# A fused attention and feed-forward kernel: one written-out order of operations for the whole first chunk

## The chip, the core and the metric

The kernel runs as one program on one core of a Trainium2 chip. The metric is the device time of one execution in microseconds. The engines named here are TensorE (PE, with its weight loads as PEld), VectorE (DVE), ScalarE (ACT), GpSimd (POOL) and SyncE (SP), which here issues nearly all DMA transfers. Each engine works through its own queue in the order in which the program hands instructions out; an instruction that waits for another engine holds up all that stand behind it on its own.

## The reference

Sparse attention over 4 batches of 8 heads, 576 positions and 64 columns a head, and then two feed-forward layers over the 2304 resulting rows of 512 columns:

```
def _attn_ref(q, k, v):
    scores = (1.0 / np.sqrt(D)) * np.matmul(q, k.transpose(0, 1, 3, 2))
    # heads 0-3 see the last 32 positions, heads 4-7 every 32nd position
    scores = np.where(masks[None], scores, -1000000000.0)
    attn = np.exp(scores - np.max(scores, axis=-1, keepdims=True))
    attn = attn / (np.sum(attn, axis=-1, keepdims=True) + 1e-09)
    return np.matmul(attn, v)

h = x @ w_in                      # 512 -> 2048
x = (h - np.tanh(h)) @ w_out      # 2048 -> 512
g = x @ w_gate                    # 512 -> 1536
x = (g / (1.0 + np.exp(-g)) * (x @ w_val)) @ w_out2
```

The inputs are float32; q and k are drawn eight times larger than in the base recipe.

## The kernel before

The 2304 rows are cut into five chunks, four of 512 and one of 256. The first feed-forward layer runs chunk by chunk, and while one chunk is multiplied, the attention of the next batch is computed beside it. The second layer follows and isn't touched by the change.

**Attention in groups.** A batch has 4 pairs of heads, and a pair 3 groups of 3 blocks of 64 queries: 12 groups a batch. Groups 0 to 11 are batch 0, groups 12 to 23 batch 1. A group goes through `scores` (PE: small matmuls), `top` (DVE: mask and row maximum, into SBUF), `exp` (ACT), `recip` (DVE), `mult` (POOL, or ACT in three instructions), `turn` (PE: three transposes into PSUM), `bring` (a copy of 384 columns from PSUM to SBUF, DVE or ACT), `value` (PE: small matmuls) and `keep` (ACT: a copy to SBUF). For groups 13 to 23 all `scores` write one part of a PSUM bank, all `turn` a second and all `value` a third, so each waits for the reader of the one before it.

**Weights in pieces.** The first layer's weights arrive as 32 pieces of 64-bit words and are turned into float32 by steps on three engines: `words` (SP: the load, into one of five buffers), `high` and `low` (ACT), `bound` (two DVE instructions, L177 and L181), `join` (POOL, L188), `sign` (DVE, L192), `head` (ACT, L198) and `rest` (POOL, L201). The last two split each weight into a high and a low part; a product takes three matmuls of 512 columns (high by high, low by high, high by low). Piece steps are the largest item on DVE and POOL in the first chunk.

**The first chunk.** Column block f of the hidden layer (f from 0 to 15) takes `first` (PE, 12 matmuls into a bank), `tanh` (ACT), `less` (DVE), `gh` (ACT) and `gl` (DVE), and then `second` (PE, 12 matmuls into four accumulators, the first eight of which read `gh` alone). This, the groups of batch 1 and the pieces are interleaved, which I call a round for each f.

**What sets the order.** Two things before the change. The text `BEGIN` is a list of such operations, written `verb.index.option`; `Opening.run` reads it word by word and hands the instructions out in that order (`warm.12` is twelve idle-time matmuls on PE; `ready` the same into a bank that a group will use; `part`, `half` and `first.i.f.n` are matmuls of the first layer; `.P`, `.V` and `.A` name POOL, DVE and ACT). It covers batch 0, and f up to 4. From f = 5 (`FROM`) the loop over `f` at the end of the kernel takes over with a fixed order: normalise the last group, `first`, `tanh`, `less`, a `value`, a `scores`, a tick of the piece feed, `second` of f-1, a `turn` and its `bring`, `gh`, `gl`, `exp`, and a second tick. A tick (`Feed.tick`) does `high` and `low` of one piece, `bound` and `join` of the one before and `sign`, `head`, `rest` of the one before that. In both, the sums of `second` for f = 15 are left to the end of the chunk, after the inputs of chunk 1 have been split.

The functions of `Opening` that read the list, and the loop:

Of the kernel before, what the change touches and what calls it, by code (L numbers as in the profile page):

```python
# [63 lines left out]
BEGIN = """
scores.0 top.0 exp.0.n warm.12 recip.0 mult.0.P keys.0.1 scores.1 scores.2 top.1 turn.0 top.2 exp.1.c queries.0.1
values.0.0 recip.1 warm.6 exp.2.n warm.6 words.0 keys.0.2 scores.3 scores.4 bring.0.V recip.2 mult.1.P turn.1 top.3
mult.2.P exp.3.c value.0 top.4 keep.0 queries.0.2 mask bring.1.V turn.2 scores.5 value.1 exp.4.n warm.12 bring.2.V
top.5 recip.3 mult.3.P recip.4 turn.3 keep.1 piece.0.high mult.4.P exp.5.c value.2 piece.0.low keep.2 piece.0.bound
bring.3.V turn.4 high.2 scores.6 bring.4.V recip.5 top.6 scores.7 values.0.1 words.1 top.7 scores.8 exp.6.n
piece.0.join piece.0.sign exp.7.c value.3 recip.6 piece.1.high mult.5.P low.2 turn.5 warm.12 keep.3 piece.1.low  # L70
bring.5.V words.2 ready.99.2 recip.7 top.8 exp.8.n mult.7.P warm.6 piece.1.bound value.4 keep.4 turn.7 keys.0.3
queries.0.3 mult.6.P bring.7.V turn.6 value.5 recip.8 piece.1.join piece.1.sign piece.0.head piece.2.high keep.5
scores.10 values.0.2 scores.9 scores.11 bring.6.V value.6 mult.8.P high.3 piece.0.rest ready.8.6 turn.8 low.3
piece.1.head words.3 xh.6 piece.1.rest top.9 top.10 exp.10.n values.0.3 xl.6 value.7 piece.2.bound words.4 words.5
keys.1.0 recip.10 top.11 ready.9.6 exp.9.c recip.9 mult.9.P xh.7 xl.7 piece.3.high mult.10.P ready.11.2 part.0.2
part.0.3 bring.8.V exp.11.c piece.3.low part.1.2 piece.3.bound recip.11 value.8 xh.8 left.8 xl.8 turn.9 turn.10
bring.9.V mult.11.A bring.10.V part.1.3 piece.3.join queries.1.0 value.9 values.1.0 keys.1.1 piece.2.low queries.1.1
piece.2.join xh.9 piece.4.high turn.11 piece.3.sign piece.3.head xl.9 part.0.0 bring.11.V value.10 value.11
piece.5.high xh.10 xh.11 piece.4.bound part.1.0 values.1.1 xl.11 left.11 first.3.2.1 xl.10 piece.4.low piece.5.low
words.6 scores.12 piece.2.sign piece.2.head piece.3.rest piece.5.bound half.0.0 half.0.1 words.7 piece.4.join tanh.0  # L80
top.12 piece.2.rest half.1.0 less.0 scores.13 half.1.1 first.3.2.11 piece.4.sign exp.12.c top.13 gh.0 gl.0
piece.5.join exp.13.c scores.14 second.2.0.8 tanh.1 piece.5.sign piece.5.head recip.12 recip.13 tanh.2 words.8 words.9
piece.4.head second.2.0.4 mult.12.P mult.13.P top.14 less.1 gh.1 second.4.1.1 less.2 piece.6.high gl.1 piece.5.rest
piece.6.rebase turn.12 piece.4.rest exp.14.c piece.6.low bring.12.V piece.7.high piece.7.low first.5.3.12 recip.14
piece.8.high piece.8.low piece.7.bound value.12 gh.2 scores.15 piece.6.join piece.6.sign piece.6.head top.15 exp.15.c
piece.9.high gl.2 tanh.3 mult.14.P turn.13 second.4.1.7 piece.7.join words.10 words.11 spill.5 piece.8.bound
piece.7.sign second.4.1.4 piece.6.rest recip.15 piece.8.join bring.13.V piece.9.bound second.6.2.8 piece.8.sign
keep.12 value.13 piece.7.head keys.1.2 queries.1.2 piece.7.rest piece.10.high mult.15.P piece.9.low scores.16
piece.9.join turn.14 less.3 second.6.2.4 bring.14.V top.16 words.12 gh.3 first.7.4.1 piece.10.bound keep.13
piece.9.sign gl.3 first.7.4.11 turn.15 bring.15.V piece.8.head piece.8.rest piece.10.low words.13 second.8.3.1  # L90
piece.11.low piece.11.high tanh.4 second.8.3.11 piece.10.join piece.11.bound words.14 piece.10.sign piece.9.head
piece.9.rest spill.8 exp.16.c less.4 piece.12.high piece.10.head words.15 gh.4 piece.11.join piece.13.high
# [1660 lines left out]
```

## Time and profile before

| | us |
|---|---|
| median of three runs | 866.4 (866.13 to 866.54) |
| the profiled execution | 866.65 |
| its span, first to last instruction | 864.8 |
| PE busy in the span | 858.8 |
| DVE busy | 639.5 |
| ACT busy | 463.5 |
| POOL busy | 334.9 |

Times in the rows below are counted from the start of the span. An engine's busy time is the union of its instructions as the profiler records them; ends of matmuls are modelled, and matmuls overlap, so a row of PE is read by the start of the next one. The opening lasts to about 28 us, where the first wide matmul starts; chunk 0 ends on PE at 138.43 us.

### The profile page before, as it was taken

The page shows a single profiled execution, that of the slowest core. Times are in us where ns is not written, and L with a number is a line of the kernel's source. Part 1 is how long each engine was busy: PE and PEld are TensorE (multiplying, and loading weights), DVE is VectorE, ACT ScalarE, POOL GpSimd, SP SyncE. Part 2 cuts the span into 40 slices and gives each one's busy share as a digit, 9 for nine tenths or more (in the row PEclk, how much of TensorE's full clock was granted, in tenths as well). Part 3 has the DMA queues.
Part 4 walks back from the last instruction along what each step waited for, and adds up shares of the span by engine and source line. Part 5 has one row for each costly group of instructions (what it writes and reads, how often), then busy time and mean ns, then how long its engine had stood idle before and what let it go on. Part 6 is the DMA issues. An engine that isn't in the chain of part 4 may idle for free.

```text
span 864.8 us, 13917 instructions
## 1 busy us (share of the span) xinstructions
PE 858.8 (99%) x4782; PEld 720.3 (83%) x4782; DVE 639.5 (74%) x1218; ACT 463.5 (54%) x1059; POOL 334.9 (39%) x284
## 2 busy tenths in 40 slices
PE   9999999999999999999999999999999999999998
PEld 7877778888888889998888888888888888888886
DVE  6999996688867785248887887888777867785451
ACT  6988874534343524237644655655454446854531
POOL 3889994754546550005125214463553310000000
PEclk9999999999999999999999999999999999999999
DMA  9967646530352213247356436453444458978651
GB/s 267 293 236 243 197 165 203 211 98 25 128 191 91 74 50 122 98 150 250 137 171 217 148 121 199 145 196 143 160 159 170 165 203 307 372 250 274 197 186 42
DMA packets 67253, 152.47 MB, mean 176 GB/s; under 512 B 7600, under 2 KB 14128, under 8 KB 67184
## 3 DMA queue, kind: packets, MB, share of 16 engines
q1 hardware_dynamic: 66752, 151.35, 52.1%
q8 instruction: 37, 0.61, 0.3%
q10 hardware_dynamic: 432, 0.25, 0.1%
q14 instruction: 32, 0.26, 0.1%
HBM read 108.06 MB, written 43.52 MB: 175 GB/s over the span
## 4 chain that ended last, share of the span: by engine, by line
PE 89%; ACT 5%; DVE 4%; issue 1%; DMA 0%; POOL 0%; SPq 0%; POOLq 0%
PE ps_acc L627 17%; PE ps_h L252 8%; PE ps_h L251 8%; PE ps_h L253 8%; PE ps_acc L253 8%; PE ps_acc L252 8%; PE ps_acc L251 8%; PE ps_a L252 5%; PE ps_a L251 5%; PE ps_a L253 5%; PE ps_acc L1626 2%; DVE m L192 2%; ACT s L368 1%; PE ps_a L414 1%; PE ps_a L343 1%
## 5 line engine op out<-in xcount | busy, mean ns | idle before, releaser
L627 PE MATMUL ps_acc<-gh,w 128*128 128x512 f32 (+1 forms) x546 | 124.8, 370 | 0.0
L188 POOL TENSOR_TENSOR sl<-sl,st 128x512 int32<-128x512 int32 x36 | 51.4, 1434 | 164.9 <-PE ps_acc L627 73.6
L251 PE MATMUL ps_acc<-sl 128*128 128x512 f32 x288 | 112.1, 389 | 0.0
L252 PE MATMUL ps_acc<-sl 128*128 128x512 f32 x288 | 112.1, 389 | 0.0
L253 PE MATMUL ps_acc<-sl 128*128 128x512 f32 x288 | 112.0, 389 | 0.0
L627 PEld LDWEIGHTS ps_acc<-gh,w 128*128 128x128 f32 x546 | 94.1, 189 | 16.0
L1213 DVE TENSOR_TENSOR sl<-sl 128x512 fp32r<-128x512 f32 (+1 forms) x120 | 71.7, 660 | 22.9 <-ACT sl L1209 22.9
L251 PE MATMUL ps_h<-xh,w 128*128 128x512 f32 (+1 forms) x226 | 85.1, 376 | 0.0
L252 PE MATMUL ps_h<-xh,w 128*128 128x512 f32 (+1 forms) x226 | 84.4, 374 | 0.1
L253 PE MATMUL ps_h<-xl,w 128*128 128x512 f32 (+1 forms) x226 | 84.2, 372 | 0.0
L1209 ACT CAST sl<-sl 128x512 fp32r<-128x512 f32 (+1 forms) x120 | 66.1, 599 | 23.9 <-DMA sl<-gd 18.2
L607 ACT ACTIVATE t<-ps_h 128x512 f32<-128x512 f32 (+1 forms) x54 | 30.4, 563 | 83.2 <-PE ps_h L253 83.2
L466 POOL TENSOR_TENSOR pr<-skv,sq 128x576 f32<-128x576 f32 (+8 forms) x40 | 57.4, 1461 | 44.5 <-DVE sc L473 31.5
L627 PE MATMUL ps_acc<-gl,w 128*128 128x512 f32 (+1 forms) x273 | 67.1, 366 | 0.0
L608 DVE TENSOR_TENSOR ps_h<-ps_h,t 128x512 f32<-128x512 f32 (+1 forms) x54 | 35.5, 657 | 40.3 <-ACT t L607 40.0
L253 PEld LDWEIGHTS ps_acc<-sl 128*128 128x128 f32 x288 | 54.1, 188 | 11.2
L252 PEld LDWEIGHTS ps_acc<-sl 128*128 128x128 f32 x288 | 54.1, 188 | 11.1
L251 PEld LDWEIGHTS ps_acc<-sl 128*128 128x128 f32 x288 | 54.1, 188 | 11.0
L466 POOL TENSOR_TENSOR pr<-skv,sc 128x576 f32<-128x576 f32 (+8 forms) x40 | 45.9, 1164 | 37.7 <-DVE xo L473 28.1
L251 PE MATMUL ps_a<-sl 128*128 128x512 f32 x144 | 56.1, 390 | 0.0
L252 PE MATMUL ps_a<-sl 128*128 128x512 f32 x144 | 56.1, 390 | 0.0
L253 PE MATMUL ps_a<-sl 128*128 128x512 f32 x144 | 56.0, 389 | 0.0
(207 smaller groups left out, 2096.3 us busy)
## 6 DMA issues: line engine op xcount, KB each, us to landing
st<-in_w SPq DMA_DIRECT2D x68, 512.0 KB, 4.5
gd<-t SPq DMA_DIRECT2D x84, 256.0 KB, 2.2
sl<-gd SPq DMA_DIRECT2D x84, 256.0 KB, 4.7
w<-w1s SPq DMA_DIRECT2D x32, 512.0 KB, 3.5
w3s<-sl SPq DMA_DIRECT2D x24, 256.0 KB, 3.2
sl<-w3s SPq DMA_DIRECT2D x24, 256.0 KB, 5.3
x2d<-o SPq DMA_DIRECT2D x17, 256.0 KB, 2.7
w1s<-w SPq DMA_DIRECT2D x8, 512.0 KB, 5.3
```

The lines of the kernel that those rows point to most:

```text
L188: nc.gpsimd.tensor_tensor(out=mi, in0=mi, in1=self.lo, op=ALU.add)
L192: nc.vector.scalar_tensor_tensor(out=mi, in0=self.hi, scalar=-2 ** 30, in1=mi, op0=ALU.bitwise_and, op1=ALU.bitwise_or,)
L251: nc.tensor.matmul(ps, lhsT=wh, rhs=xh, start=start, stop=False, skip_group_check=goes_on)
L252: nc.tensor.matmul(ps, lhsT=wl, rhs=xh, start=False, stop=False, skip_group_check=goes_on)
L253: nc.tensor.matmul(ps, lhsT=wh, rhs=xl, start=False, stop=stop, skip_group_check=goes_on)
L466: nc.gpsimd.tensor_tensor(out=t, in0=x, in1=y, op=ALU.mult)
L607: nc.scalar.activation(t[:, :n], ps[:, :n], AF.Tanh)
L608: nc.vector.tensor_tensor(out=ps[:, :n], in0=ps[:, :n], in1=t[:, :n], op=ALU.subtract)
L627: nc.tensor.matmul(acc[m][:, :n], lhsT=w[:, i, m * P:(m + 1) * P], rhs=(gl if low else gh)[:, :n], start=start and not low and i == 0, sto ...
L1209: nc.scalar.copy(got[0][:, 0, :n], got[0][:, 1, :n].bitcast(F32))
L1213: nc.vector.tensor_tensor(out=w[:, 1, :n], in0=w[:, 1, :n].bitcast(F32), in1=w[:, 0, :n].bitcast(F32), op=ALU.subtract)
L1626: nc.tensor.matmul(acc[m], lhsT=lhsT, rhs=w[:, i, :], start=u == 0 and lhsT is zh and i == 0, stop=u == NF2 - 1 and lhsT is zl)
```

## The change

The list `BEGIN` now holds the whole first chunk, to `second` of f = 14 and the last group's `keep`, and the loop over f is empty for chunk 0 (`FROM` is 16). Each operation that the loop handed out stands in the list once, with its loads, its stores of streamed weights (`spill`) and the bookkeeping of their buffers, for which `Opening` gets two functions (`used`, `restore`). The part of the list that was there is in a new order too: twelve idle-time matmuls come before the first scores, for instance. The `bring` of groups 0, 6, 11, 14, 15, 16, 17, 19 and 22 is done by ACT instead of DVE, and the `mult` of groups 16, 17, 19, 22 and 23 by ACT instead of POOL. The lists are shown in part:

```diff
 BEGIN = """
-scores.0 top.0 exp.0.n warm.12 recip.0 mult.0.P keys.0.1 scores.1 scores.2 top.1 turn.0 top.2 exp.1.c queries.0.1
-values.0.0 recip.1 warm.6 exp.2.n warm.6 words.0 keys.0.2 scores.3 scores.4 bring.0.V recip.2 mult.1.P turn.1 top.3
-mult.2.P exp.3.c value.0 top.4 keep.0 queries.0.2 mask bring.1.V turn.2 scores.5 value.1 exp.4.n warm.12 bring.2.V
-top.5 recip.3 mult.3.P recip.4 turn.3 keep.1 piece.0.high mult.4.P exp.5.c value.2 piece.0.low keep.2 piece.0.bound
-bring.3.V turn.4 high.2 scores.6 bring.4.V recip.5 top.6 scores.7 values.0.1 words.1 top.7 scores.8 exp.6.n
...
-piece.13.low piece.10.rest piece.12.bound gl.4 piece.12.low piece.12.join piece.11.sign
+restore keys.0.1 queries.0.1 warm.12 values.0.0 words.0 scores.0 top.0 scores.1 exp.0.n top.1 warm.6 recip.0 exp.1.c
+scores.2 top.2 warm.6 mult.0.P keys.0.2 queries.0.2 turn.0 exp.2.n recip.1 scores.3 mult.1.P mask top.3 scores.4
+bring.0.A values.0.1 recip.2 exp.3.c words.1 turn.1 value.0 words.2 top.4 mult.2.P bring.1.V turn.2 exp.4.n recip.3
+value.1 mult.3.P bring.2.V scores.5 keep.0 recip.4 piece.0.high turn.3 keys.0.3 value.2 piece.0.low top.5 mult.4.P
+queries.0.3 piece.0.bound exp.5.c values.0.2 turn.4 scores.6 words.3 scores.7 top.6 piece.0.join keep.2 warm.12 keep.1
...
+piece.1.low piece.1.bound value.5 bring.7.V scores.10 piece.2.high values.0.3 recip.8 piece.1.join scores.9 bring.6.A
...
+value.9 mult.11.A piece.2.sign value.10 turn.11 xh.9 piece.3.sign xh.10 part.1.0 bring.11.A xl.10 piece.3.head
...
+gh.1 scores.14 piece.4.rest top.14 piece.5.head turn.12 scores.15 piece.6.low gl.1 second.2.0.4 piece.7.high less.2
...
+used.5.0 piece.8.rest piece.11.bound bring.14.A spill.8 piece.10.sign piece.12.high piece.11.join words.15 gh.4
...
+piece.13.sign values.1.2 piece.15.low piece.14.join piece.15.bound words.18 mult.16.A piece.13.head scores.18
+piece.12.rest keep.14 top.18 gh.5 turn.16 scores.19 tanh.6 piece.14.sign value.15 piece.16.high piece.13.rest less.6
...
+piece.16.bound piece.17.high bring.16.A keep.15 piece.15.join mult.17.A top.19 first.13.7.12 used.7.0 gh.6
...
+piece.19.high first.15.8.12 used.8.0 recip.18 piece.19.low piece.19.bound mult.18.P spill.16 bring.17.A piece.18.join
...
+piece.23.low piece.23.bound piece.22.join first.21.11.12 tanh.10 mult.19.A less.10 piece.23.join piece.25.high
+piece.22.sign mult.20.P turn.19 piece.22.head words.27 value.18 spill.21 scores.22 piece.22.rest keep.18 bring.19.A
...
+top.23 restore used.13.0 mult.22.A piece.28.bound piece.27.rest piece.29.high piece.29.low turn.22 piece.29.bound
...
+bring.22.A exp.23.c less.13 piece.29.sign second.26.12.12 used.12.1 restore used.14.0 gh.13 piece.28.sign
+piece.29.head gl.13 piece.31.high piece.29.rest piece.28.head tanh.14 piece.28.rest first.29.15.12 spill.29
+piece.31.low piece.31.bound recip.23 less.14 mult.23.A piece.30.join piece.31.join value.22 tanh.15 turn.23
...
+less.15 keep.22 piece.31.head gl.14 value.23 piece.31.rest second.30.14.12 used.14.1 keep.23 gh.15 spill.31 gl.15
 """
-FROM, AT, HELD, MADE = 5, 14, 11, []
+FROM = 16
...
+            def restore(self):
+                restore()
+
+            def used(self, f, part):
+                used(0, (f, part))
...
         x, order = opening.x, PAIRS
-        feed1.at = AT
-        feed1.held = HELD
-        feed1.made = [(at, feed1.pieces[i]) for at, i in MADE]
```

## Rows read from the trace of the kernel before

**Rows 1.** The page, part 1: busy time of each engine, its share, instructions.
```profile
PE 858.8 (99%) x4782; PEld 720.3 (83%) x4782; DVE 639.5 (74%) x1218; ACT 463.5 (54%) x1059; POOL 334.9 (39%) x284
```

**Rows 2.** Busy time by stage: stretch and length, each engine's busy us (instructions), PEclk, DMA.
```profile
8.00:28.00 20.00, 19.44 (x292) 16.18 (x291) 18.23 (x98) 18.41 (x68) 13.44 (x15) 1.00 0.94 270
60.00:118.00 58.00, 57.86 (x404) 45.12 (x403) 56.90 (x126) 48.94 (x131) 52.99 (x43) 1.00 0.71 220
```

**Rows 3.** Timeline of PE in the opening: start, length, line, operation, count, [idle before].
```profile
1.10 3.17 PE L658 MATMUL ps_h<-warm 128*128 128x256 bf16 x14 [1.10 <-POOL warm L653]
4.53 1.06 PE L351 MATMUL ps_acc<-kt,qt 64*64 64x80 f32 x12 [0.26 <-DMA kt<-in_k]
5.53 1.56 PE L658 MATMUL ps_h<-warm 128*128 128x256 bf16 x12
...
8.42 0.53 PE L402 MATMUL ps_acc<-ident_sb,s 128*80 128x128 f32 x3 [0.35 <-POOL s L386]
...
25.97 0.49 PE L402 MATMUL ps_acc<-ident_sb,s 128*96 128x128 f32 x3
26.39 0.57 PE L414 MATMUL ps_a<-pt,vt 96*64 96x64 f32 x12
...
27.69 0.48 PE L251 MATMUL ps_h<-xh,w 128*128 128x512 f32 x1
```

**Rows 4.** Timeline of ACT in the opening.
```profile
7.98 0.36 ACT L368 ACTIVATE s<-s,mx 128x80 f32<-128x80 f32 x1 [1.20 <-DVE mx L359]
```

**Rows 5.** Timeline of PE in the rounds, and chunk 1's first matmul (last row).
```profile
92.33 0.57 PE L414 MATMUL ps_a<-pt,vt 96*64 96x64 f32 x12
...
99.34 0.57 PE L414 MATMUL ps_a<-pt,vt 96*64 96x64 f32 x12
99.73 0.67 PE L351 MATMUL ps_a<-kt,qt 128*64 128x96 f32 x12
...
106.48 0.57 PE L414 MATMUL ps_a<-pt,vt 96*64 96x64 f32 x12
...
113.60 0.57 PE L414 MATMUL ps_a<-pt,vt 96*64 96x64 f32 x12
...
120.70 0.57 PE L414 MATMUL ps_a<-pt,vt 96*64 96x64 f32 x12
...
138.43 0.39 PE L251 MATMUL ps_h<-xh,w 128*128 128x512 f32 x1
```

**Rows 6.** The chain of waits: start, length, what.
```profile
88.45 1.57 DVE m L192
...
95.58 1.57 DVE m L192
```

**Rows 7.** Timeline of DVE, one `top` and the copy behind it.
```profile
97.05 0.24 DVE L359 CUSTOM_DVE_ANT_0 s<-ps_a,mask_l 128x96 f32<-128x96 f32 x1
...
97.58 0.54 DVE L406 COPY pt<-ps_a 96x384 f32<-96x384 f32 x1
98.05 0.67 DVE L615 TENSOR_TENSOR gl<-ps_h,gh 128x512 fp32r<-128x512 f32 x1
```

**Rows 8.** Timeline of POOL at the same place.
```profile
95.30 1.29 POOL L201 TENSOR_TENSOR w<-m,w 128x512 fp32r<-128x512 f32 x1
```

**Rows 9.** Groups by line up to 138.5 us: count | busy us, mean ns | idle before.
```profile
L424 ACT COPY x<-ps_a 128x192 f32<-128x192 f32 x18 | 5.6, 311 | 0.5 <-DVE mx L359 0.3
...
L614 ACT CAST gh<-ps_h 128x512 fp32r<-128x512 f32 x6 | 3.5, 582 | 0.3 <-DVE ps_h L608 0.3
...
L393 ACT ACTIVATE s<-s,sm 128x96 f32<-128x96 f32 x3 | 0.9, 367 | 0.1
...
L386 POOL TENSOR_TENSOR s<-s,sm 128x288 f32<-128x288 f32 x11 | 7.7, 708 | 0.5 <-DVE sm L381 0.3 <-ACT x L424 0.2
```

**Rows 10.** Instructions on tile `m`, 60 to 118 us: duration ns min/median/max.
```profile
L192 DVE SCALAR_TENSOR_TENSOR m<-st,m x17: 681/686/1565, 61.4 to 116.9; 128x512 int32<-128x512 int32 x17
```

**Rows 11.** Waits of ACT, 60 to 136 us: total us, times, longest.
```profile
ACT w L198 <- DVE m L192: 11.2, 11, 1.5
```

More of the change, by code (lines that the diff above doesn't have):

```diff
@@ L70 @@
[L70 to L89, printed above, removed]
@@ new lines @@
+value.4 mult.6.P recip.7 keep.3 warm.12 bring.5.V high.2 top.8 mult.7.P exp.8.n ready.99.2 low.2 turn.7 turn.6
+piece.1.low piece.1.bound value.5 bring.7.V scores.10 piece.2.high values.0.3 recip.8 piece.1.join scores.9 bring.6.A
+words.4 keep.4 top.9 words.5 warm.6 keys.1.0 top.10 mult.8.P scores.11 queries.1.0 piece.1.sign ready.8.6
+piece.2.bound piece.2.low keep.5 piece.0.head exp.10.n piece.0.rest turn.8 piece.1.head ready.9.6 high.3 piece.1.rest
+value.6 value.7 bring.8.V ready.11.2 xh.6 xh.7 part.0.2 low.3 xl.6 xl.7 recip.10 exp.9.c value.8 part.1.2 top.11
@@ new lines @@
+values.1.0 mult.10.P piece.3.high keys.1.1 recip.9 part.0.3 xh.8 mult.9.P queries.1.1 left.8 piece.3.low piece.3.bound
+turn.10 piece.2.join turn.9 exp.11.c xl.8 part.0.0 bring.9.V piece.3.join part.1.3 piece.4.high recip.11 bring.10.V
+value.9 mult.11.A piece.2.sign value.10 turn.11 xh.9 piece.3.sign xh.10 part.1.0 bring.11.A xl.10 piece.3.head
+piece.4.bound value.11 first.3.2.1 piece.3.rest xh.11 values.1.1 piece.5.high scores.12 words.6 piece.2.head xl.11
+half.0.1 xl.9 words.7 piece.4.low half.0.0 piece.2.rest words.8 half.1.0 piece.5.low piece.5.bound scores.13 tanh.0
@@ new lines @@
+top.12 piece.4.join half.1.1 less.0 first.3.2.11 tanh.1 top.13 gh.0 piece.5.join less.1 exp.12.c gl.0 piece.5.sign
+left.11 second.2.0.8 tanh.2 recip.12 piece.4.sign piece.6.high mult.12.P words.9 piece.4.head piece.6.rebase words.10
+gh.1 scores.14 piece.4.rest top.14 piece.5.head turn.12 scores.15 piece.6.low gl.1 second.2.0.4 piece.7.high less.2
+piece.5.rest exp.13.c second.4.1.1 second.4.1.7 piece.6.join piece.7.low piece.7.bound recip.13 piece.8.high mult.13.P
+first.5.3.12 piece.6.sign gh.2 piece.9.high piece.7.join top.15 words.11 piece.6.head bring.12.V spill.5 piece.9.bound
@@ new lines @@
+keys.1.2 piece.9.low piece.6.rest queries.1.2 piece.8.low turn.13 value.12 exp.14.c piece.7.sign scores.16
+piece.9.join bring.13.V second.4.1.4 words.12 gl.2 piece.7.head second.6.2.8 tanh.3 piece.8.bound piece.7.rest
+exp.15.c piece.9.sign first.7.4.1 piece.8.join top.16 second.6.2.4 piece.9.head recip.15 recip.14 piece.10.high less.3
+first.7.4.11 piece.11.low piece.9.rest piece.10.bound piece.10.low gh.3 mult.14.P keep.12 piece.8.sign piece.11.high
+piece.10.join turn.14 gl.3 words.13 tanh.4 scores.17 words.14 piece.8.head value.13 less.4 exp.16.c first.9.5.12
@@ new lines @@
+used.5.0 piece.8.rest piece.11.bound bring.14.A spill.8 piece.10.sign piece.12.high piece.11.join words.15 gh.4
+piece.12.bound keep.13 second.8.3.1 piece.10.head second.8.3.11 mult.15.P piece.13.high recip.16 gl.4 piece.10.rest
+piece.12.low top.17 piece.13.low piece.11.sign tanh.5 second.10.4.12 used.4.1 restore piece.12.join piece.14.high
+words.16 less.5 piece.11.head piece.13.bound exp.17.c piece.11.rest piece.12.sign piece.14.low value.14 piece.13.join
+piece.14.bound piece.15.high turn.15 words.17 first.11.6.12 used.6.0 keys.1.3 piece.12.head queries.1.3 bring.15.A
@@ new lines @@
+piece.13.sign values.1.2 piece.15.low piece.14.join piece.15.bound words.18 mult.16.A piece.13.head scores.18
+piece.12.rest keep.14 top.18 gh.5 turn.16 scores.19 tanh.6 piece.14.sign value.15 piece.16.high piece.13.rest less.6
+words.19 piece.14.head gl.5 second.12.5.12 used.5.1 restore piece.16.low piece.14.rest recip.17 spill.13
+piece.16.bound piece.17.high bring.16.A keep.15 piece.15.join mult.17.A top.19 first.13.7.12 used.7.0 gh.6
+piece.16.join exp.18.c piece.17.low piece.17.bound piece.15.sign piece.16.sign words.20 turn.17 tanh.7 scores.20
@@ new lines @@
+piece.17.join gl.6 words.21 piece.18.high value.16 less.7 piece.15.head second.14.6.12 used.6.1 restore piece.17.sign
+piece.16.head gh.7 piece.15.rest words.22 keep.16 piece.18.low piece.18.bound piece.16.rest piece.17.head gl.7
+piece.19.high first.15.8.12 used.8.0 recip.18 piece.19.low piece.19.bound mult.18.P spill.16 bring.17.A piece.18.join
+piece.20.high top.20 exp.19.c piece.17.rest turn.18 value.17 tanh.8 scores.21 piece.19.join piece.20.low
+piece.20.bound first.17.9.12 less.8 piece.21.high piece.18.sign gh.8 piece.20.join piece.18.head words.23 values.1.3
@@ new lines @@
+exp.20.c piece.18.rest second.16.7.12 used.7.1 restore used.9.0 tanh.9 piece.21.low piece.21.bound piece.19.sign
+piece.20.sign words.24 piece.22.high piece.21.join less.9 keep.17 words.25 piece.20.head gl.8 second.18.8.12 used.8.1
+restore piece.19.head recip.20 piece.21.sign piece.22.low piece.19.rest gh.9 bring.18.V words.26 top.21 piece.21.head
+piece.22.bound exp.21.c piece.20.rest first.19.10.12 used.10.0 gl.9 piece.21.rest piece.23.high recip.19 piece.24.high
+piece.23.low piece.23.bound piece.22.join first.21.11.12 tanh.10 mult.19.A less.10 piece.23.join piece.25.high
@@ new lines @@
+piece.22.sign mult.20.P turn.19 piece.22.head words.27 value.18 spill.21 scores.22 piece.22.rest keep.18 bring.19.A
+second.20.9.12 used.9.1 restore used.11.0 piece.25.low piece.24.low piece.24.bound top.22 piece.23.sign recip.21
+piece.25.bound piece.23.head words.28 gh.10 piece.23.rest piece.26.high gl.10 turn.20 tanh.11 value.19 bring.20.V
+piece.24.join piece.26.low scores.23 piece.26.bound piece.27.high second.22.10.12 used.10.1 restore piece.25.join
+less.11 piece.24.sign piece.26.join piece.24.head words.29 first.23.12.12 used.12.0 exp.22.c piece.25.sign mult.21.P
@@ new lines @@
+words.30 gh.11 piece.26.sign piece.25.head piece.24.rest keep.19 piece.27.low piece.27.bound turn.21 value.20 spill.24
+gl.11 second.24.11.12 used.11.1 keep.20 piece.27.join tanh.12 words.31 piece.28.high less.12 piece.28.low
+piece.25.rest bring.21.V gh.12 recip.22 piece.26.head piece.27.sign first.25.13.12 piece.26.rest gl.12 piece.27.head
+top.23 restore used.13.0 mult.22.A piece.28.bound piece.27.rest piece.29.high piece.29.low turn.22 piece.29.bound
+value.21 piece.30.high piece.28.join first.27.14.12 piece.30.low keep.21 piece.30.bound tanh.13 piece.29.join
@@ new lines @@
+bring.22.A exp.23.c less.13 piece.29.sign second.26.12.12 used.12.1 restore used.14.0 gh.13 piece.28.sign
+piece.29.head gl.13 piece.31.high piece.29.rest piece.28.head tanh.14 piece.28.rest first.29.15.12 spill.29
+piece.31.low piece.31.bound recip.23 less.14 mult.23.A piece.30.join piece.31.join value.22 tanh.15 turn.23
+second.28.13.12 used.13.1 restore used.15.0 piece.30.sign piece.31.sign piece.30.head bring.23.V gh.14 piece.30.rest
+less.15 keep.22 piece.31.head gl.14 value.23 piece.31.rest second.30.14.12 used.14.1 keep.23 gh.15 spill.31 gl.15
```

4 lines of the change are left out of this document (1 added, 3 removed).

## The prediction

> **What bounds the kernel now.** I read the page first, then the busy time by stage, the chain of waits, the queues in order of time, and last the waits by engine. The page gives PE as busy for 99% of the span [rows 1]. Ends of matmuls are modelled, so this alone proves nothing; the steps from one start to the next do. Chunk 1 begins on PE at 138.43 us [rows 5]; nothing that the change touches runs later, so all of it is decided before. There the stages differ. From 8 to 28 us PE (19.4 of 20 us), DVE (18.2) and ACT (18.4) are all nearly full [rows 2], PE being filled with idle-time matmuls. From 60 to 118 us, the rounds of the first chunk, PE shows 57.86 of 58 us, DVE 56.90, POOL 52.99, ACT 48.94 [rows 2]: PE and DVE run neck and neck. The chain of waits says which one leads: one `sign` on DVE (L192) stands in it at 88.45 and its successor at 95.58, 7.13 us on [rows 6], while PE comes round in 7.01 us when nothing holds it (92.33 to 99.34) and in 7.14 and 7.12 us in the next two rounds [rows 5]. So DVE paces the later rounds by a hair, and PE is only just behind. That is the first limit of this change: PE has the same matmuls before and after, and it idles little. What could be won at all is the sum of its small waits.
>
> **The change part by part.** Counted over the list and the loop that it replaces, each operation stands as often as before; only 9 copies go from DVE to ACT and 5 multiplications from POOL to ACT.
>
> *Engine loads.* A copy takes DVE 0.47 us (97.58 to 98.05) [rows 7]; nine free it of 4.2 us. A multiplication takes POOL 0.71 us [rows 9]; five are 3.5 us. On ACT no such copy of 384 columns is shown; one of 192 took 0.31 and one of 512 took 0.58 us [rows 9]. Those are the ends, I take 0.47 between them. The one multiplication on ACT, of three rows at 0.37 us, is 0.9 us as the group's busy time shows [rows 9]. So ACT gets 9 x 0.47 + 5 x 0.9 = 8.7 us. Its cover: between 60 and 136 us it waited 11.2 us in 11 places for `sign` on DVE [rows 11], and most of the added work lies there. Direct cost 0. Without that cover it would be at most 8.7 us; this is the third rival.
>
> *The opening.* Twelve fill-in matmuls are moved ahead of the first scores. The first fourteen step at 0.21 us, the twelve at 5.53 at about 0.11 (1.56 us in all with the last one's length), half the time, with the change at about 5.7 us [rows 3]; the granted clock reads 1.00 for the whole stage from 8 us on [rows 2]. From 4.1 us some seven of the moved ones go at 0.21 and five at 0.11: the first scores begin at 6.2 instead of 4.53 us. Against this, the scores themselves then run at the full step (0.5 instead of 1.06 us) and the twelve no longer stand behind them. Before, the next scores began behind the row of 5.53 us that lasts 1.56, at 7.0 us; now they begin at 6.7: -0.3. The first transposes waited 0.35 us at 8.42 for POOL [rows 3]. Their multiplication depends on the first scores, which are 1.7 us late, less 0.6 for the faster scores: 9.5 us. PE, with two groups of scores and twelve fill-ins from 6.7 on (0.5 each, and 1.3), is there at 9.0; wait 0.5, so +0.15. The second exponential began at 7.98 after a wait of 1.20 for its scores [rows 4]; those now come directly behind the first, so ACT starts it at 8.0 as before, and ACT's queue is not late. One step is worse: the third reciprocal now stands behind `top.3` on DVE, which needs the fourth scores; I charge one `top`, 0.53 us (97.05 to 97.58) [rows 7], to the third transposes. Sum -0.3 + 0.15 + 0.53 = +0.4. Ends: -0.9 (the 0.3, PE's waits of 0.35 and 0.26 us [rows 3], and nothing new) and +1.7 (all of the first delay survives).
>
> *The rounds.* With 4.2 us taken off DVE the loop between DVE and ACT no longer paces. What PE lost to it: 0.13 and 0.11 us in two rounds, and in that from 113.60 to 120.70 us, which lasts 7.10 though it has no scores any more (0.67 us for a group [rows 5], so 6.4 were due), about 0.7. Sum 0.9, taken at -0.9. Ends: 0 and -1.3 (another 0.04 in each of ten rounds).
>
> *New waits.* `scores.14` and `scores.15`, and `scores.18` and `scores.19`, now stand one behind the other with only a group of transposes between, and both write the same part of a bank: the second must wait for the `top` of the first. A `top` lasts 0.53 us [rows 7], the transposes cover 0.42 us of it from their start to the next one (25.97 to 26.39) [rows 3]; that leaves 0.11 each at least, and the whole 0.53 where DVE is still busy with other things when the scores end. I take 0.25 each, +0.5. Ends 0 and +1.1 (two `top`s bare). Behind the waiting scores PE holds a group of values and a wide run of matmuls; nobody else waits for it.
>
> *PE's order.* After the first wide matmul, small ones come in 19 stretches instead of 28. A wide matmul behind small ones is 0.48 us long (27.69) [rows 3] where one in a run is 0.39 (138.43) [rows 5], so nine fewer are up to -0.8. But groups that now meet other small ones lose the cover of a wide run behind them; no row prices that, so I set this end as large, +0.8, and take 0, the middle.
>
> *SP, POOL.* Loads keep their order on SP. A weight load waits for the `sign` five pieces earlier, and in the new list that comes earlier against its use, so 0. POOL's queue loses five steps; 0 while PE leads. Chunk 1's splitting starts when the last first-layer matmul has run; three more groups and a wide run now stand behind that one, so it has more room: 0.
>
> Sum: +0.4 - 0.9 + 0.5 + 0 = 0.0 us. The profiled execution took 866.65 us with a span of 864.8, 0.25 above the median of 866.4; so **866.4 us** is the forecast. All good ends together give -0.9 - 1.3 + 0 - 0.8 = -3.0, all bad ones +1.7 + 0 + 1.1 + 0.8 = +3.6.
>
> **A rule against it.** A `sign` takes 0.68 us at best and 1.57 at worst, median 0.69 of 17 [rows 10]. The long ones begin just after a `rest` on POOL: 95.58 against 95.30, and DVE is free again at 97.05, after the `rest` of 1.29 us has ended at 96.6 [rows 6 to 8]. The Trainium skill ("SBUF — State Buffer", section "Who interferes with whom") says that a DVE instruction with two inputs in SBUF contends with a GpSimd one that reads it, and that the second to issue blocks fully until the first ends. By that rule, and the trace agrees, what a `sign` costs depends on where the new order puts it against POOL. As many blocked as now leave the sum at 0.0; more of them make the second rival.
>
> **The rivals.** *DVE relieved, nothing new* (31%): new waits stay hidden, the opening is no later, PE runs through. For it: DVE's 7.13 us against PE's 7.01; against it: the first scores at 6.2 us. It takes -0.5 in the opening, -1.3 in the rounds and -0.6 of PE's order: -2.4, 864.0 us. It cannot be much more, since PE has no more idle time to give.
>
> *More signs blocked* (16%; slower). Place: DVE in the rounds. Of the 17 between 60 and 118 us about half are long now (ACT waited 11 times for one up to 136 us [rows 11]); the new list runs pieces in pairs with both signs side by side, so that either can fall on a `rest`. Each further long one costs 1.57 - 0.69 = 0.88 us of DVE [rows 10]; its relief in the rounds is six copies, 2.8 us, so from four more it paces harder than now. With eight, +7.0 - 2.8 = +4.2, of which the rounds' old loss of 0.9 is already paid: about +3.3, 869.7 us. Against it: POOL has 3.5 us less to do.
>
> *ACT becomes the bound* (8%). From 60 to 118 us it has 48.94 us [rows 2]; five copies and four multiplications more make 54.9 of 58. If the halves for the second layer then come late by one such step, 0.5 us, in five rounds: +2.5, 868.9 us.
>
> **How the numbers follow.** The forecast, no change, gets 45%. A measurement of this kernel tells 0.2% from nothing, 1.7 us; so faster means under 864.7 and slower over 868.1. Faster 31% (first rival), same 45%, slower 24% (second and third). The likeliest case by itself spans 865.0 to 868.0; with the others, the range is 863.8 to 869.5.
>
> **What would show it.** First scores at 6.2 us; the first wide matmul near 28 us; rounds of 7.0 us with no step of PE held between 100 and 121 us; short waits of PE at the second of two scores on one bank. First matmul of chunk 1 near 138.4 us. The forecast is wrong if that comes before 136.7 or after 140.1; a count of long `sign`s above 12 in the rounds would speak for the second rival, ACT without gaps there for the third.

## The result, and the profile after

The changed kernel takes **875.2 us** in the median (874.2 to 875.8) against 866.4 us: 8.8 us slower, ratio 1.0101 with an interval of 1.0084 to 1.0119. I had forecast 866.4, in a range up to 869.5.

The profiled execution took 875.78 us with a span of 873.9, 9.1 more than before. All of it is lost before chunk 1: its first matmul stands at 147.54 us instead of 138.43 [rows 5], 9.11 later. First the busy times, whole and by stage, beside [rows 1, 2]:

```profile
PE 861.6 (99%) x4782; PEld 721.7 (83%) x4782; DVE 630.9 (72%) x1209; ACT 469.8 (54%) x1083; POOL 328.6 (38%) x279
...
8.00:28.00 20.00, 18.66 (x277) 14.59 (x273) 16.52 (x92) 17.47 (x60) 11.86 (x14) 1.00 0.90 264
60.00:118.00 58.00, 53.97 (x370) 42.74 (x369) 48.57 (x108) 48.65 (x132) 46.58 (x36) 0.97 0.65 210
```

The page still says 99% for PE. The stage shows it: 57.86 of 58 us have become 53.97. And no other engine has taken PE's place. DVE fell from 56.90 to 48.57, POOL from 52.99 to 46.58, and ACT, with work added, stayed at 48.65 (48.94 before). PE, DVE and POOL all stand idle more than before, so what grew is waiting of one queue for another. The timeline of PE names its places (in brackets, the idle time before the row and what ended it); compare [rows 3, 5]:

```profile
5.85 1.05 PE L383 MATMUL ps_acc<-kt,qt 64*64 64x80 f32 x24
...
9.31 0.53 PE L434 MATMUL ps_acc<-ident_sb,s 128*80 128x128 f32 x3 [0.33 <-POOL s L418]
...
12.64 0.53 PE L434 MATMUL ps_acc<-ident_sb,s 128*80 128x128 f32 x3 [0.87 <-POOL s L418]
...
28.61 0.48 PE L283 MATMUL ps_h<-xh,w 128*128 128x512 f32 x1
...
46.12 0.64 PE L383 MATMUL ps_a<-kt,qt 128*64 128x80 f32 x12 [1.00 <-DVE mx L391]
...
71.84 0.52 PE L434 MATMUL ps_a<-ident_sb,s 128*80 128x128 f32 x3 [1.39 <-DVE m L213]
...
76.94 0.72 PE L383 MATMUL ps_a<-kt,qt 128*64 128x96 f32 x12 [0.71 <-DVE mx L391]
...
112.38 0.50 PE L434 MATMUL ps_a<-ident_sb,s 128*96 128x128 f32 x3 [1.88 <-DVE m L213]
...
114.64 2.76 PE L842 MATMUL ps_acc<-gh,w 128*128 128x512 f32 x6
...
135.04 0.50 PE L829 MATMUL ps_h<-xh,w 128*128 128x512 f32 x1 [0.59 <-POOL w L233]
...
147.54 0.39 PE L283 MATMUL ps_h<-xh,w 128*128 128x512 f32 x1
```

(L383 is `scores`, L434 `turn`, L213 the second instruction of `bound`, L391 `top`, L233 `rest`; the change moved all line numbers down by 32.) The six long waits are at turn.2 (0.87), scores.15 (1.00), turn.15 (1.39), scores.19 (0.71), turn.20 (1.88) and first.29 (0.59): 6.4 us. A wait of a `turn` for a `bound` needs explaining, since transposes use nothing that `bound` makes. DVE at both places:

```profile
70.39 0.68 DVE L209 SCALAR_TENSOR_TENSOR m<-m,ps_a 128x512 f32<-128x512 f32 x1
71.10 0.69 DVE L213 SCALAR_TENSOR_TENSOR m<-m,ps_a 128x512 int32<-128x512 int32 x1
...
108.31 0.69 DVE L209 SCALAR_TENSOR_TENSOR m<-m,ps_a 128x512 f32<-128x512 f32 x1 [2.05 <-ACT pt L438]
109.03 0.69 DVE L213 SCALAR_TENSOR_TENSOR m<-m,ps_a 128x512 int32<-128x512 int32 x1
...
111.55 0.69 DVE L213 SCALAR_TENSOR_TENSOR m<-m,ps_a 128x512 int32<-128x512 int32 x1
```

`bound` reads `ps_a`. Two banks have that name: one holds the scores and the values of groups 13 to 23, the other their transposes and, in columns 504 and 505, the two limits that `bound` reads. In these rows a write to a bank waits for the readers ahead of it in the list, whatever columns they read. turn.15 begins at 71.84, when the `bound` from 71.10 has ended (71.79); turn.20 at 112.38, when the one from 111.55 has (112.24). And the tie works the other way. At 108.31 a `bound` had waited 2.05 us for a copy on ACT (L438, `bring`) that only reads the same bank. On ACT that copy had stood behind a `keep` that waited for scores (first PE, then ACT):

```profile
106.47 0.57 PE L446 MATMUL ps_a<-pt,vt 96*64 96x64 f32 x12
106.86 0.67 PE L383 MATMUL ps_a<-kt,qt 128*64 128x96 f32 x12
...
107.58 0.32 ACT L456 COPY x<-ps_a 128x192 f32<-128x192 f32 x1 [0.67 <-PE ps_a L383]
107.79 0.48 ACT L438 COPY pt<-ps_a 96x384 f32<-96x384 f32 x1
```

The `keep` reads only the `value` of 106.47 (L446), done at 107.04; it waited for the scores behind that (107.53), which use the same bank. From 108.31 DVE works without a gap up to the `bound` that turn.20 needs. So the 1.88 us of PE at 112 come from a chain through both banks: a `keep` late on ACT through the bank of scores and values, a copy late behind it, then through the bank of the transposes a `bound` late on DVE and the next transposes late on PE. The Trainium skill ("PSUM — Partial Sum Buffer", section "PSUM bank collisions raise a hardware error") says that the compiler's scheduler adds a dependency between any two instructions on different engines that touch the same bank in the same 32 partitions, reads against reads included. These rows agree: ACT's copies and DVE's `bound`s, both readers, waited for each other 3.5 and 2.6 us (second and third row below, 60 to 136 us; the first shows how little ACT now waits for a `sign`, 3 times against 11 [rows 11]; the last is all `sign`s from 60 to 128 us).

```profile
ACT w L230 <- DVE m L224: 4.1, 3, 1.8
ACT pt L438 <- DVE m L213: 3.5, 4, 1.5
```
```profile
DVE m L209 <- ACT pt L438: 2.6, 2, 2.1
```
```profile
L224 DVE SCALAR_TENSOR_TENSOR m<-st,m x18: 658/686/1787, 62.9 to 124.0; 128x512 int32<-128x512 int32 x18
```

The account of the 9.1 us: PE's idle time between its first scores and the end of the chunk's matmuls, summed over every gap in the trace, grew from 0.7 to 7.2 us, +6.5. Behind the longest wait the granted clock fell (0.51 in the stretch from 114 to 116 us), and the twelve matmuls from 113.81 to 118.24 took 4.4 us, where the same twelve a round later took 2.9 (121.88 to 124.74): +1.6. Some 1.0 us are left, spread over starts of short matmuls; no run isolates them. The loss doesn't need the fall of the clock: the three other executions of the changed kernel took 874.2 to 875.7 us at a mean granted clock of 0.999 to 1.000.

### The profile page after: what moved, and what is told of

It reads as the page before. It is cut to its first block, busy times and chain, and to the rows that moved or that the text cites. A ratio compares the mean times of both kernels' runs of the same rounds, so it can differ in the third digit from the quotient of the medians.

```text
span 873.9 us, 13930 instructions
## 1 busy us (share of the span) xinstructions
PE 861.6 (99%) x4782; PEld 721.7 (83%) x4782; DVE 630.9 (72%) x1209; ACT 469.8 (54%) x1083; POOL 328.6 (38%) x279
## 4 chain that ended last, share of the span: by engine, by line
PE 94%; ACT 2%; DVE 2%; issue 1%; POOL 1%; DVEq 0%; ACTq 0%; POOLq 0%
PE ps_acc L659 17%; PE ps_h L283 8%; PE ps_h L285 8%; PE ps_h L284 8%; PE ps_acc L284 8%; PE ps_acc L283 8%; PE ps_acc L285 8%; PE ps_a L284 5%; PE ps_a L283 5%; PE ps_a L285 5%; PE ps_acc L842 2%; PE ps_acc L1661 2%; PE ps_acc L829 2%; PE ps_h L829 2%; PE ps_a L446 2%; PE ps_a L375 1%
## 5 line engine op out<-in xcount | busy, mean ns | idle before, releaser
L659 PE MATMUL ps_acc<-gh,w 128*128 128x512 f32 (+1 forms) x480 | 107.8, 367 | 0.0
L659 PEld LDWEIGHTS ps_acc<-gh,w 128*128 128x128 f32 x480 | 81.7, 189 | 13.2
L283 PE MATMUL ps_h<-xh,w 128*128 128x512 f32 (+1 forms) x202 | 75.3, 373 | 0.0
L284 PE MATMUL ps_h<-xh,w 128*128 128x512 f32 (+1 forms) x202 | 74.8, 370 | 0.0
L285 PE MATMUL ps_h<-xl,w 128*128 128x512 f32 (+1 forms) x202 | 74.8, 370 | 0.0
L639 ACT ACTIVATE t<-ps_h 128x512 f32<-128x512 f32 (+1 forms) x48 | 26.9, 561 | 81.2 <-PE ps_h L285 81.2
L285 PEld LDWEIGHTS ps_acc<-sl 128*128 128x128 f32 x288 | 54.1, 188 | 11.2
L640 DVE TENSOR_TENSOR ps_h<-ps_h,t 128x512 f32<-128x512 f32 (+1 forms) x48 | 31.3, 652 | 42.0 <-ACT t L639 41.8
L659 PE MATMUL ps_acc<-gl,w 128*128 128x512 f32 (+1 forms) x240 | 57.9, 363 | 0.0
```

The lines of the kernel that those rows point to most:

```text
L283: nc.tensor.matmul(ps, lhsT=wh, rhs=xh, start=start, stop=False, skip_group_check=goes_on)
L284: nc.tensor.matmul(ps, lhsT=wl, rhs=xh, start=False, stop=False, skip_group_check=goes_on)
L285: nc.tensor.matmul(ps, lhsT=wh, rhs=xl, start=False, stop=stop, skip_group_check=goes_on)
L639: nc.scalar.activation(t[:, :n], ps[:, :n], AF.Tanh)
L640: nc.vector.tensor_tensor(out=ps[:, :n], in0=ps[:, :n], in1=t[:, :n], op=ALU.subtract)
L659: nc.tensor.matmul(acc[m][:, :n], lhsT=w[:, i, m * P:(m + 1) * P], rhs=(gl if low else gh)[:, :n], start=start and not low and i == 0, sto ...
```

## The experiments

Each was timed beside the kernel before; the time of that was 866.3 to 866.6 us in all of them. The runs in the old order have its loop over f written out as a list. That by itself costs nothing: the run with two copies moved has it too, and takes 865.9 us.

| run | us | ratio (interval) |
|---|---|---|
| changed kernel | 875.2 | 1.0101 (1.0084 to 1.0119) |
| order alone, nothing more on ACT | 875.2 | 1.0096 (1.0080 to 1.0111) |
| moves to ACT alone, old order | 874.0 | 1.0083 (1.0070 to 1.0096) |
| old order, nine copies | 870.9 | 1.0046 (1.0030 to 1.0063) |
| old order, five multiplications | 869.7 | 1.0034 (1.0021 to 1.0047) |
| old order, the one copy bring.15 | 868.8 | 1.0028 (1.0016 to 1.0039) |
| old order, the two copies bring.6 and 14 | 865.9 | 0.9992 (0.9983 to 1.0001) |
| old opening, new rounds | 873.5 | 1.0089 (1.0074 to 1.0104) |
| new opening, old rounds | 870.1 | 1.0045 (1.0030 to 1.0060) |
| new list, two words moved | 875.1 | 1.0095 (1.0082 to 1.0109) |
| new list, six words moved | 874.1 | 1.0085 (1.0072 to 1.0097) |
| new list, `bound`s and `turn`s moved | 872.2 | 1.0064 (1.0050 to 1.0077) |
| old order, limits in the scores' bank | 875.1 | 1.0103 (1.0088 to 1.0118) |
| old order, limits in SBUF | 904.8 | 1.0441 (1.0426 to 1.0457) |
| new list, limits in SBUF | 906.2 | 1.0458 (1.0442 to 1.0474) |

**Order or moves?** The two halves of the change apart:

```
# order alone: the new list with every bring.*.A as .V and the five mult.*.A as .P
# moves alone: the kernel before, its loop written out as a list, with those .A
```


> The new list with all nine copies back on DVE and the five multiplications back on POOL: the order alone. Theory 1 (waits between queues, made by the order): most of the loss stays, 872 to 877 us. Theory 2 (ACT too full): the loss goes with the 7.6 us of work that ACT gets rid of, 866 to 869 us.

> The order of the kernel before, written out as one list (its loop unrolled), with the nine copies and five multiplications on ACT: the moves alone. Theory 1: the order is the loss, the moves alone cost little: 865 to 869 us; what may remain is that a copy on ACT and the `bound`s on DVE, which read the same bank, wait for each other. Theory 2 (ACT too full): 872 to 877 us.

Each half costs nearly as much as both. That clears ACT's load in the new list: in sum, taking the added work away changes nothing (PE's idle time stays at 7.2 us, in part at other places). It does not clear the moves, which cost 7.4 us by themselves in the old order. My first two theories were both half wrong, and the sizes don't add.

**Single words.** In the changed list, first the two `turn`s (the order of every queue stays), then six words:

```
- value.14 piece.13.join piece.14.bound piece.15.high turn.15
+ value.14 piece.13.join turn.15 piece.14.bound piece.15.high
...
- recip.21 piece.25.bound ... gl.10 turn.20
+ recip.21 turn.20 piece.25.bound ... gl.10
```
```
# the second run, besides these two
- top.3 scores.4 bring.0.A values.0.1 recip.2
+ scores.4 bring.0.A values.0.1 recip.2 top.3
...
- turn.12 scores.15 piece.6.low gl.1 second.2.0.4
+ turn.12 piece.6.low gl.1 second.2.0.4 scores.15
...
- scores.18 piece.12.rest keep.14
+ keep.14 scores.18 piece.12.rest
...
- exp.23.c ... piece.29.head
+ piece.29.head exp.23.c ...
```


> The changed kernel with two words of the list moved up: turn.15 ahead of piece.14.bound and turn.20 ahead of piece.25.bound. No engine's own order of instructions changes by this, only what waits for what. Theory 1 (waits between queues): the clamp's limits that `bound` reads lie in the same bank as the transposes, so a `turn` has to wait for every `bound` that stands ahead of it in the list; these two waited 1.39 and 1.88 us in the changed kernel, and go. It expects both waits under 0.2 us and 871 to 873 us. Theory 2 (ACT is too full with the nine copies and five multiplications): no queue changes, so 874 to 876 us. Theory 3 (the new list as such keeps PE's matmuls from overlapping): 874 to 876 us.

> The changed kernel with six words moved, one for each long wait of PE: turn.15 and turn.20 ahead of the `bound`s, keep.14 ahead of scores.18, scores.15 behind second.2.0.4, top.3 behind recip.2, piece.29.head ahead of exp.23.c. The nine copies and five multiplications stay on ACT. Theory 1: the six waits (1.39, 1.88, 0.71, 1.00, 0.87 and 0.59 us, together 6.4) go, and with them the loss: 867 to 870 us. Theory 2 (ACT too full): no less than 873 us, since new waits for ACT take their place.

Both missed. The two waits went, as said (0.25 us are left at turn.15, nothing at turn.20), and the time stayed, since others came. PE's waits in the first run, 8 to 145 us (all us, times, longest), then in the second:

```profile
PE ps_a L434 <- DVE m L213: 2.7, 2, 2.4
PE ps_acc L434 <- POOL s L418: 1.2, 2, 0.9
PE ps_a L383 <- DVE mx L391: 1.1, 2, 0.8
...
```
```profile
PE ps_a L434 <- DVE m L213: 2.4, 1, 2.4
PE ps_a L383 <- ACT x L456: 1.4, 1, 1.4
...
```

The 2.4 us now stand at turn.21, the next one with a `bound` ahead of it; the 1.4 us at scores.18, which I had put behind keep.14 to save 0.7 elsewhere. It was DVE that was late, and moving a `turn` doesn't change that. In the first run DVE, then PE:

```profile
108.10 0.69 DVE L209 SCALAR_TENSOR_TENSOR m<-m,ps_a 128x512 f32<-128x512 f32 x1 [2.06 <-ACT pt L438]
...
119.19 0.69 DVE L213 SCALAR_TENSOR_TENSOR m<-m,ps_a 128x512 int32<-128x512 int32 x1
```
```profile
120.02 0.51 PE L434 MATMUL ps_a<-ident_sb,s 128*96 128x128 f32 x3 [2.43 <-DVE m L213]
```

DVE stood 2.06 us for the copy on ACT, as in the changed kernel, and worked without a gap from 108.10 to the `bound` that turn.21 needs, with three `sign`s in 3.60 us among that work. turn.20 passes ahead of that queue, and the delay reaches PE at the next `turn`.

**The limits out of PSUM.** The tie goes if the limits lie in SBUF:

```
-    limits = banks[1][:, 504:506]
+    limits = const.tile([P, 2], F32, name="limits")
```


> The changed kernel with the two limits that `bound` reads in SBUF and no longer in the bank of the transposes; the list stays. Theory 1a (it is the shared bank that ties `turn`, `bring` and `bound` together, across three queues): all waits of a `turn` for a `bound`, of a copy on ACT for a `bound` and of a `bound` for a copy go, which moving single words only shifted to the next place: 867 to 871 us. Theory 4 (the new list gives DVE and POOL their work in bursts, and PE waits at the end of each, whatever the path): 873 to 876 us. Should `bound` itself be slower from SBUF beside POOL, its rows of 0.69 us grow, and it is over 876 us; the next run prices that.

> The order of the kernel before (all on DVE and POOL as there) with the two limits of `bound` in SBUF: the price of that edit by itself. In the old order no `turn` waits for a `bound`, so theories 1a and 4 both expect nothing from the bank: 866 to 867 us if the place of the limits is free; 870 us or more, with rows of `bound` above 0.69 us, if DVE then stands behind POOL more often.

This could not tell the theories apart, since the edit has a price of its own of 38 us. In the old order, 60 to 118 us (ns min/median/max):

```profile
L234 POOL TENSOR_TENSOR w<-m,w x13: 1473/1732/2211, 60.3 to 114.9; 128x512 fp32r<-128x512 f32 x13
L214 DVE SCALAR_TENSOR_TENSOR m<-m,limits x13: 694/1650/1678, 60.9 to 114.4; 128x512 int32<-128x512 int32 x13
```

The second half of `bound` goes from 689 ns (its median in the kernel before) to 1650, `rest` from 1.29 us [rows 8] to 1.73. This is what the place in PSUM saves: with the limits in SBUF `bound` has two inputs there, as a `sign` has, and stands behind POOL as a `sign` does. The rule of the Trainium skill that the prediction weighed ("SBUF — State Buffer", section "Who interferes with whom") says so of any DVE instruction with two inputs in SBUF, and these rows agree.

**The same tie at another bank.** So I kept the limits in PSUM and changed the bank, in the old order:

```
-    limits = banks[1][:, 504:506]
+    limits = banks[0][:, 504:506]
```


> The order of the kernel before, all copies and multiplications where they were there, and one index changed: the two limits that `bound` reads lie in the bank of the scores and values (columns 504 and 505) and no longer in that of the transposes. No instruction is added, dropped or moved in any queue, and `bound` still reads PSUM, so it is as fast as it was. Theory 1 (the shared bank ties queues: PE's write to it waits for every `bound` ahead of it in the list, and a `bound` for the write ahead of it): now each group of scores and of values waits for `bound`, some thirty places, most hidden, those of the opening up to a pair of 1.36 us: 870 to 878 us, and the waits of PE name `bound` at the lines of scores or values. Theory 4 (only how the queues are filled counts, not the bank): 866 to 867 us.

875.1 us: the digit costs 8.8 us, as much as the whole change, with every queue holding the same instructions in the same order. PE's waits, 8 to 145 us (L447 `value`, L384 and L376 `scores`, L214 `bound`, L457 `keep`):

```profile
PE ps_a L447 <- DVE m L214: 3.3, 3, 1.9
PE ps_acc L384 <- DVE pt L439: 1.2, 1, 1.2
PE ps_a L376 <- DVE m L214: 0.8, 1, 0.8
PE ps_a L447 <- ACT x L457: 0.6, 1, 0.6
...
```

Values and scores now wait for `bound`, of which they use nothing: 4.1 of PE's 7.3 us of idle time name it, and `bound` itself takes what it took (689 ns). It is shown by this that ties through a bank can make a loss of this size; not yet that they make it in the changed list.

**Copies and multiplications by themselves.**

> The order of the kernel before, and of the moves only the nine copies on ACT. Theory 5 (a copy at the head of ACT's queue waits for its transposes, and the halves for the next pieces stand behind it): nearly the whole 7.4 us of both moves, 871 to 875 us. Theory 2 (it is ACT's load): in proportion to the work, 3.5 of 7.6 us, so about 870 us.

> The order of the kernel before, and of the moves only the five multiplications on ACT. Theory 5: a multiplication waits for nothing that is late, so 866 to 868 us. Theory 2 (ACT's load): 4.1 of 7.6 us, so about 870.5 us.

Nine copies cost 4.5 us and five multiplications 3.3: nearer to load than to my theory 5, by the sums. The traces say otherwise. With the multiplications alone (DVE, and ACT ahead of it):

```profile
66.56 0.70 DVE L856 TENSOR_TENSOR ps_h<-ps_h,t 128x512 f32<-128x512 f32 x1 [1.42 <-ACT t L852]
67.16 0.68 DVE L210 SCALAR_TENSOR_TENSOR m<-m,ps_a 128x512 f32<-128x512 f32 x1
67.87 0.69 DVE L214 SCALAR_TENSOR_TENSOR m<-m,ps_a 128x512 int32<-128x512 int32 x1
```
```profile
65.17 0.87 ACT L426 ACTIVATE s<-s,sm 128x80 f32<-128x80 f32 x3 [0.28 <-DVE sm L414]
65.95 0.58 ACT L852 ACTIVATE t<-ps_h 128x512 f32<-128x512 f32 x1
```
```profile
PE ps_a L435 <- DVE m L214: 3.1, 5, 1.0
```

In the old order the multiplication stands directly ahead of `tanh` (L852). Its 0.87 us make `less` (L856) late, `less` makes the `bound`s behind it late, and the `turn` waits for these through the bank, at 16, 17, 19, 22 and 23, the five groups that were moved, and nowhere else: 3.1 us in five waits, for a run that lost 3.3. ACT had room for the work. It was put on a chain with little to spare: for turn.16 in the kernel before, the last `bound` ended at 67.52 us and the transposes began at 68.05:

```profile
66.83 0.69 DVE L181 SCALAR_TENSOR_TENSOR m<-m,ps_a 128x512 int32<-128x512 int32 x1
...
68.05 0.49 PE L402 MATMUL ps_a<-ident_sb,s 128*80 128x128 f32 x3
```

For the copies I took one, and then two:

> The order of the kernel before, and one single copy on ACT: bring.15. Theory 5 (head of the queue): ACT comes to it 2.7 us before its transposes are done and the `head` of piece 8 and the halves of pieces 10 and 11 stand behind it, for which second.8 then waits 1.1 and 0.9 us, as in the run with all nine copies: 868 to 870 us from this one copy. Theory 2 (ACT's load): a ninth of what the nine copies cost, 866.5 to 867 us.

> The order of the kernel before, with two copies on ACT, bring.6 and bring.14, at which ACT comes when their transposes are done or nearly so. Theory 5 (a copy costs only where it holds up ACT's queue): 865.4 to 866.5 us, no loss and perhaps half a microsecond won by DVE. Theory 2 (load, two ninths of the 4.5 us of all nine): 867.3 us.

One copy of nine makes 2.5 of the 4.5 us, and two others nothing, as theory 5 expected of both runs. What the nine cost beyond the one goes with the clock: their four executions took 868.8 us at a mean granted clock of 1.000, and 870.3 to 872.2 at 0.997 or 0.998. ACT comes to bring.15 when its transposes haven't run, 2.16 us early, with `head` of piece 8 behind it; second.8 on PE then waits for that `head` and for the `rest` after it:

```profile
58.62 0.47 ACT L439 COPY pt<-ps_a 80x384 f32<-80x384 f32 x1 [2.16 <-PE ps_a L435]
58.99 0.62 ACT L231 CAST w<-m 128x512 fp32r<-128x512 f32 x1
```
```profile
59.66 0.50 PE L843 MATMUL ps_h<-gh,w 128*128 128x512 f32 x1 [1.08 <-ACT w L231]
61.02 0.80 PE L843 MATMUL ps_h<-gh,w 128*128 128x512 f32 x1 [0.86 <-POOL w L234]
```

With bring.6 and bring.14 on ACT the run takes 865.9 us, the only time below the kernel before, by 0.5 us, with an interval that just reaches no change. ACT was early there too:

```profile
54.36 0.48 ACT L439 COPY pt<-ps_a 80x384 f32<-80x384 f32 x1 [1.25 <-PE ps_a L435]
```

But nothing that stood behind it was needed soon: PE's only wait from 8 us on is one of 0.4 us at 8.1. So neither load nor coming early is the price of a copy; what counts is whether PE soon needs what stands behind it.

**Opening or rounds?** With the cut at first.3.2.11 (38 us):

> The opening of the kernel before (its words up to the first whole run of wide matmuls, at 38 us) with its copies on DVE, and behind it the changed kernel's order, copies and multiplications. The changed kernel was 1.35 us late at 38 us and 9.2 us late at the end of the first chunk. If the rounds lose what they lost there, 872 to 875 us; if the late opening pushed the rest out of step (its waits are consequences), 866 to 869 us.

> The other half: the changed kernel's opening up to 38 us, with its three copies on ACT there, and behind it the rounds in the order of the kernel before with all on DVE and POOL. Expected from the trace: the 1.35 us of the opening and little else, 867 to 869 us; if the late opening pushes the rounds out of step too, 871 us or more.

The new rounds alone lose 7.2 us, with the same waits at the same words (turn.15, scores.19, turn.20, first.29), so they are not a consequence of the late opening. The new opening loses 3.8, more than the 1.35 us of late start that I expected; in its profiled run the 26 fill-in matmuls at the start also took 5.73 us, not 4.82 as in the changed kernel's, and scores.14 waited 0.7 us.

**The ties in the changed list.**

```
- piece.22.sign mult.20.P turn.19 piece.22.head ... keep.18 bring.19.A
+ piece.22.sign mult.20.P piece.22.head ... keep.18 turn.19 bring.19.A
- mult.22.A piece.28.bound piece.27.rest ... turn.22 piece.29.bound value.21
+ piece.28.bound piece.27.head ... mult.22.A turn.22 piece.27.rest ... value.21
...
```


> The changed kernel with ACT's and POOL's queues and the fourteen moved copies and multiplications as they are; moved in the list are sixteen `bound`s (8, 10, 11, 13, 14, 16, 19, 21, 26, 28 to 31 among them) and nine `turn`s with one `value`, so that a `turn` stands ahead of the `bound`s that DVE does later, and top.3 behind recip.2 and scores.15 behind second.2.0.4. Theory 1 (ties through the bank of transposes and limits, and the two in-order waits): about half of the 8.8 us comes back, 869.5 to 872 us, with no wait of a `turn` over 1 us. Theory 2 (ACT's load) and a theory that the order of ACT and POOL is at fault: 874 to 876 us, since neither queue changes.

(What was moved is thirteen `bound`s and not sixteen, and six `turn`s.) 872.2 us, 0.2 over what theory 1 expected: 3.0 of the 8.8 us come back with ACT's and POOL's queues untouched, PE's idle time falling from 7.2 to 5.0 us. The longest waits that remain are mostly of another kind:

```profile
PE ps_a L446 <- ACT x L456: 1.4, 1, 1.4
...
PE ps_a L434 <- ACT s L400: 0.7, 1, 0.7
PE ps_a L434 <- DVE m L213: 0.4, 1, 0.4
...
```

The first is a `value` waiting for the `keep` of the group before, which still reads the place that it overwrites; the prediction looked for waits of that kind. Two of the edits, top.3 and scores.15, took out waits of 0.87 and 1.00 us (0.28 came back behind the first), so the 3.0 us aren't all of the bank; what `bound` and `turn` brought lies between 1.4 and 3.0. No wait of a `turn` for a `bound` is over 0.44 us any more. How the other 5.8 us divide between further ties and DVE's work coming in bursts stays open.

## Why the prediction was wrong

**The step that failed is "New waits", +0.5 (0 to +1.1).** In its place PE's idle time grew by 6.5 us in the profiled execution. I looked for waits by data: which instruction needs whose result or buffer. That found scores.15 and scores.19, and under-priced both (1.00 and 0.71 instead of 0.25 each). The `top` that scores.15 needs stood on DVE behind an instruction of piece 6 that took 1.55 us beside POOL, at 44 us; the `top` that scores.19 needs had waited 1.85 us for a `keep` on ACT that reads the same bank (76.17 us), so that wait has a tie in it too. The prediction missed the waits that have no data in them. The limits of `bound` are defined one line below the bank of the transposes, as two columns of it, and I had read that line as a place for two numbers. The old order has every `bound` ahead of its `turn` by enough; the new list puts `bound`s directly ahead of turn.15 and turn.20. These two make 3.3 us of idle time; in the profiled execution the clock that fell behind the second took 1.6 more. How much of the loss all such ties make in the new list isn't shown beyond the 1.4 to 3.0 us that moving them gave back.

**The rounds, -0.9.** DVE was relieved as I said (its `sign`s too: ACT waited for one 3 times, not 11), and PE gained nothing: with the copies back on DVE the new order takes the same 875.2 us. I took PE and DVE running neck and neck for two loads, of which the larger sets the pace. They are one loop through three in-order queues, and a lighter DVE in another order is idle, not early.

**ACT at nothing.** The size was right: a copy of 384 columns took 0.48 us (I took 0.47), a multiplication three rows of 0.37. The cover was named wrongly. Idle time of ACT, 11.2 us [rows 11], says that there is room, not that it lies where the added work is. In the new list the moves are indeed free, in sum; in the old one the same work costs 7.4 us.

**The opening, +0.4 (to +1.7).** First scores at 5.85 us (forecast 6.2); turn.2 waits 0.87 for the cause named, `recip.2` behind `top.3` (0.53); first wide matmul at 28.61 instead of 27.69, +0.9 where +0.4 was forecast. Up to there it is right in kind and within its ends, and too small. With the old rounds behind it the new opening costs 3.8 us, above its upper end. That 5.85 lies so near to 6.2 is partly chance: in five other profiled executions that begin with the same words the first scores stand between 5.31 and 6.76 us.

**PE's order, 0 (+-0.8).** The 1.0 us left over in the account are the only trace of it, above its upper end. **POOL** at 0 holds but for first.29 (0.59).

**The rivals.** The relieved DVE (31%) and more blocked `sign`s (16%) are both refuted, the second by the count: 3 of 18 `sign`s from 60 to 128 us take over 1.2 us, where 8 of 17 did from 60 to 118; their median is 0.69 as before. ACT as the bound (8%, +2.5) comes near the five multiplications alone in the old order (+3.3), but late `bound`s made that, and not late halves; in the new list it is refuted. None had the bank in it, so even the sum of all bad ends, +3.6, was less than half of the loss.

## What to carry to other kernels

When instructions are put in a new order, list for each shared PSUM bank who touches it on which engine, constants parked in it included, and check the new order against that list as well as against the data. Price work that is moved to an engine with idle time by what stands behind it in that queue and by the slack of that chain, not by the idle sum. And where a wait is repaired by moving one word, ask which queue was late: if it stays late, the delay comes out at the next tie.
